# Attention and a four-expert layer from a build-time planner: softmax sums in a flow of their own, one region for P, one exponential per bank

## The chip, the cores and the metric

The kernel runs on one core of one Trainium2 chip. The metric is the device time of one execution in microseconds (us), as the median of the runs shown. It is a single launch; all arrays lie in device memory before and after it, and everything is 32-bit.

## What is computed

```python
q_pool = q.reshape(B, H, S // 2, 2, D).mean(axis=3)        # B=8, H=8, S=1152, D=64
attn = softmax(scale * q_pool @ k.T)                       # 576 queries x 1152 keys per head
x = (attn @ v) -> [B, 576, 512]
logits = x @ w_gate;  w = softmax of the two best of E=4 experts
for e in range(E):                                         # each expert: causal attention
    a = softmax(causal(scale * (x@wq[e]) @ (x@wk[e]).T))   # 576 x 576, head size 64
    out += (row's weight for e) * (a @ (x@wv[e]) @ wo[e])
```

## The kernel before

**Stages.** The 64 heads are worked in 32 head pairs (`p`), the two heads of a pair side by side: one in rows 0 to 63 of TensorE's array, one in rows 64 to 127. The 576 queries of a pair are two blocks (`QB`: 256 and 320), its 1152 keys nine chunks of 128 (`NKC`). For each pair the kernel

- loads K in three pieces (512, 512 and 128 columns, `f_loadk`), splits it into a high part by a cast on ACT and a low part by a subtraction on POOL (`f_prepk`), and does the same to Q;
- finds row maxima from the high parts alone: products of 512 columns into PSUM (`f_max`, `f_mxs`), reduced on DVE (`row_max`, L635);
- computes scores keys-by-queries with four products per chunk and head (high by high, low by high, high by low, and a row of ones times the negated maxima; `rows2`, L378), and takes `exp` of them from PSUM into tiles called `pt` (this is P, L725, `f_st`). A bank of 512 columns holds two chunks of the 256-query block or one chunk of the 320-query block; each chunk and head has an ACTIVATE of its own;
- multiplies P by V (`f_av`, `cols2`, L385: two matmuls a head, the heads in different columns of the array) and adds the chunk's P into the P of chunk 0 (`sacc`), so that the sum over keys needs one reduction at the end. The addition is issued in the same step as the product: on POOL (`add_up`, L397), or, if the planner's clock of POOL is over 3.0 us (`OFP`) behind and DVE's is not behind, as a folding reduction on DVE into a small tile (`fold_in`, `fold32`, L776; at most three for one block). The `pt` tile is freed behind the addition;
- at the end of a block folds the sum, inverts it through a small product (L823), scales and writes the pair's x in a high and a low part (`g_norm`, `g_split`, `f_xfin`).

After four pairs a batch's x is complete, and its experts' part starts: projections (`f_qk`, `f_vproj`, L369, all 128 rows and columns of the array), maxima (`f_mmax`), scores by chunk and query block (`f_mst`), P by V (`f_mav`) and the output product (`f_out`). In `f_mst`, for every batch but the last, chunk 1 is multiplied twice: 128 columns for queries 128 to 255 (packed in one bank with chunk 0) and 320 columns for block 1.

**Order.** The instruction order of every engine is fixed at build time by a list planner. Each stage is a Python generator (a "flow") that yields the time from which its next step can run and, for PE steps, a mode: A for products on 64-row halves (L378), B for P by V and the sums' small product (64-column halves), C for full products (L369). `emit` advances one model clock per engine. At each step the loop at the end picks a flow: what continues the present mode if it is ready within a tolerance, else by `pref()`, else what is ready first. The rules are the rows of `PLAN`: one row per half pair (65 rows, 16 numbers each). Columns 1 and 2 are how many us PE may wait for a score step or a P-by-V step (column 1 mostly 0.3 to 0.6); columns 3 and 4 are counts of waiting P-by-V steps from which mode B goes before mode C, and from which such a step has no extra 3 us. The set that is counted (`wait_av`) holds for each block only its next chunk, since only that one is asked.

**Buffers.** `pt` is a ring of 20 tiles of 2 x 320 columns, each with a tag of its own; K arrives in three 512-column tiles (`kraw`), which also take the 128-column piece; x has five buffers, and from the sixth chunk (`XG`) of a pair its x buffer must be had. PSUM's eight banks are one ring (`gen`).

Of the kernel before, what the change touches and what calls it, by code (L numbers as in the profile page):

```python
# [14 lines left out]
NB = 8  # L15
# [16 lines left out]
NPT, NKH = 20, 6  # L32
SWC = 0.8
NSL, OFP, OFD = 4, 3.0, 0.0
# [13 lines left out]
WST, WSP, WPR = 1.0, 0.2, 4  # L48
XG = 6
# [129 lines left out]
class Kept(Ring):  # L179
# [5 lines left out]
    def new(self):  # L185
        t = min(self.slots)
        self.slots.remove(t)
        self.live += 1
        r = Res(self.aps[t[3]], self)
        _, r.u, r.ue, r.slot = t  # L190
        return r

# [16 lines left out]
def pooled_attention_then_moe_kernel(ctx: ExitStack, tc: tile.TileContext, qT, kT, vP, wall, wop, out):  # L209
# [78 lines left out]
    r_x = ring("x", [128, 2, SQ], F32R, 5)  # L288
# [146 lines left out]
    KH, KL, QH, QL = {}, {}, {}, {}  # L435
    KT = lambda p: ((0, 384), (384, 384), (768, 384)) if p == 0 else ((0, 512), (512, 512), (1024, 128))
# [22 lines left out]
    wait_av, go = set(), [0]  # L459

    def av_need(key, *t):
        if key not in wait_av:
            wait_av.add(key)
# [10 lines left out]
    def av_prio():  # L474
        return 1.5 if cut[0] == "B" else 2.5 if len(wait_av) >= row(4) else 4.5
# [13 lines left out]
    def f_loadk(p, t):  # L489
        yield lambda: max(r_kraw.avail(), sp())  # L490
        k = r_kraw.new()
        a, n = KT(p)[t]
        mv(k[:, :n], kT[p, :, a:a + n], [], [k])
# [15 lines left out]

    def load_first():  # L510

        ks, (q, q1), qh, ql = [r_kraw.new() for _ in range(3)], [r_qraw.new() for _ in range(2)], r_qh.new(), r_ql.new()
# [805 lines left out]
```

## Time and profile before

| | |
|---|---|
| median of 3 runs | 1123.16 us (1123.04 to 1123.74) |
| span of the profiled execution | 1123.1 us |
| PE / DVE / POOL / ACT busy | 1092.6 / 875.7 / 874.4 / 651.9 us |
| first matmul to last | starts 7 us after the first instruction, ends 5 us before the last |

Busy times are the union of an engine's instructions in the profiled execution; the span is from its first instruction to its last, and nothing is added around it, since span and median agree to 0.1 us. A matmul's recorded duration holds its way through the array as well, so that neighbours overlap, and the distance from one start to the next tells what it costs.

### The profile page before, as it was taken

Reading aid. Unit: us, or ns where it says so; the run is one execution under the profiler, and the core shown is the slowest. Engines: PE = TensorE matmul, PEld = TensorE weight load, DVE = VectorE, ACT = ScalarE, POOL = GpSimd, SP = SyncE. Lnnn points to the kernel's source line nnn. Section 1 sums busy time; section 2 is a strip of 40 time slices with the busy share of each in tenths; the row PEclk is TensorE's granted clock in tenths of the full one; section 3 lists DMA queues with packets and bytes.
Section 4 is the critical chain, followed back from the end, with each engine's and each line's share of the span. In section 5 each row is a group of like instructions: output and inputs, shape, how many; then the busy total and the mean of one; then the engine's idle time right before and its main releaser. Section 6 shows DMA issues by size and latency. Waiting matters only on the chain.

```text
span 1123.1 us, 29516 instructions
## 1 busy us (share of the span) xinstructions
PE 1092.6 (97%) x11184; PEld 878.3 (78%) x11184; DVE 875.7 (78%) x2055; ACT 651.9 (58%) x2036; POOL 874.4 (78%) x808
## 2 busy tenths in 40 slices
PE   7998999999999999999999999999999999999997
PEld 5876798777987779778787778877787877987785
DVE  8999878787688776978578787788768887677885
ACT  5765637666375654657456674567645766456543
POOL 5898948999299991999939998399965999468812
PEclk9998999999999999999999999999999999999999
DMA  7332321223113122221322023230232203200011
GB/s 186 92 100 80 78 52 52 65 65 84 33 55 75 34 74 70 63 57 33 100 69 73 23 73 88 59 84 4 74 88 74 65 2 108 58 23 2 2 39 48
DMA packets 46398, 70.31 MB, mean 63 GB/s; under 512 B 7216, under 2 KB 25648, under 8 KB 46256
## 3 DMA queue, kind: packets, MB, share of 16 engines
q1 hardware_dynamic: 41648, 59.15, 17.2%
q0 software_dynamic: 4464, 9.14, 5.6%
q8 instruction: 88, 1.44, 0.5%
q14 instruction: 54, 0.44, 0.1%
q10 hardware_dynamic: 144, 0.13, 0.0%
HBM read 58.73 MB, written 9.44 MB: 61 GB/s over the span
## 4 chain that ended last, share of the span: by engine, by line
PE 70%; POOL 12%; DVE 11%; issue 2%; DMA 2%; ACT 2%; SPq 0%; POOLq 0%; DVEq 0%; ACTq 0%
PE gen L378 31%; PE gen L369 20%; PE gen L385 19%; POOL pt L397 10%; DVE PM L635 5%; DVE part L776 2%; DMA qraw<-in_qT 2%; POOL pt L1125 1%; DVE gen L1062 1%; POOL kl L397 1%; ACT pt L725 1%; PE gen L823 1%; DVE WL L393 1%; DVE gate L977 1%; DMA kraw<-in_kT 0%
## 5 line engine op out<-in xcount | busy, mean ns | idle before, releaser
L397 POOL TENSOR_TENSOR pt<-pt,pt 128x512 f32<-128x512 f32 (+4 forms) x488 | 667.7, 1374 | 40.5 <-PE gen L385 5.1
L635 DVE TENSOR_REDUCE PM<-gen 128x1 f32<-128x512 f32 (+3 forms) x678 | 407.8, 658 | 132.2 <-PE gen L378 107.4
L725 ACT ACTIVATE pt<-gen 128x320 f32<-128x320 f32 (+1 forms) x1152 | 371.6, 446 | 63.0 <-PE gen L378 56.3
L385 PE MATMUL gen<-pt,v 128*64 128x320 f32 (+4 forms) x2752 | 346.7, 403 | 2.0 <-POOL pt L1125 1.5
L385 PEld LDWEIGHTS gen<-pt,v 128*64 128x64 f32 (+1 forms) x2752 | 189.0, 137 | 127.9 <-issue 7.4
L378 PE MATMUL gen<-qh,kh 64*128 64x320 f32 (+1 forms) x1152 | 229.8, 312 | 4.8 <-DVE PM L635 2.5
L378 PE MATMUL gen<-qh,kl 64*128 64x320 f32 (+1 forms) x1152 | 218.1, 299 | 0.0
L378 PE MATMUL gen<-ql,kh 64*128 64x320 f32 (+1 forms) x1152 | 210.6, 293 | 0.0
L378 PE MATMUL gen<-RM,ON 64*128 64x320 f32 (+1 forms) x1152 | 210.4, 292 | 0.0
L378 PEld LDWEIGHTS gen<-qh,kh 64*128 64x128 f32 x1152 | 155.8, 186 | 28.1 <-ACT pt L725 7.3
L776 DVE TRANSPOSE_TENSOR_REDUCE part<-pt 128x20 f32<-128x640 f32 (+1 forms) x188 | 143.4, 781 | 27.5 <-POOL pt L397 27.2
L378 PE MATMUL gen<-kh,qh 64*128 64x512 f32 (+2 forms) x768 | 149.4, 374 | 11.2 <-ACT qh L389 7.1
L378 PEld LDWEIGHTS gen<-RM,ON 64*128 64x128 f32 x1152 | 149.6, 187 | 0.0
L378 PEld LDWEIGHTS gen<-ql,kh 64*128 64x128 f32 x1152 | 149.3, 186 | 0.0
L378 PEld LDWEIGHTS gen<-qh,kl 64*128 64x128 f32 x1152 | 146.1, 186 | 2.8
L397 POOL TENSOR_TENSOR kl<-kraw,kh 128x512 fp32r<-128x512 f32 (+2 forms) x96 | 103.0, 1104 | 21.0 <-PE gen L378 16.7
L378 PEld LDWEIGHTS gen<-kh,qh 64*128 64x128 f32 x768 | 88.3, 189 | 29.9 <-issue 11.2
L369 PE MATMUL gen<-x,WH 128*128 128x320 f32 (+1 forms) x512 | 105.0, 299 | 0.0
L977 POOL TENSOR_TENSOR gate<-v,gate 128x20 f32<-128x20 f32 x7 | 1.6, 225 | 123.9 <-DVE gate L977 123.9
L369 PEld LDWEIGHTS gen<-x,WH 128*128 128x128 f32 x512 | 81.9, 188 | 4.2 <-issue 1.9
L1062 DVE CUSTOM_DVE_ANT_0 gen<-gen,mqk 64x288 f32<-64x288 f32 (+4 forms) x160 | 74.3, 504 | 9.6 <-PE gen L378 8.4
L389 ACT COPY accs<-gen 128x256 f32<-128x256 f32 (+1 forms) x96 | 39.1, 407 | 70.6 <-PE gen L385 70.5
(117 smaller groups left out, 1523.3 us busy)
## 6 DMA issues: line engine op xcount, KB each, us to landing
v<-in_vP SPq DMA_DIRECT2D x96, 192.0 KB
kraw<-in_kT SPq DMA_DIRECT2D x62, 256.0 KB
qraw<-in_qT SPq DMA_DIRECT2D x31, 288.0 KB
qraw<-in_qT POOLq DMA_DIRECT2D x31, 288.0 KB, 4.5
out<-ob SPq DMA_DIRECT2D x28, 256.0 KB
kraw<-in_kT SPq DMA_DIRECT2D x31, 64.0 KB
RM<-nt SPq DMA_DIRECT2D x124, 1.2 KB
wst<-in_wall SPq DMA_DIRECT2D x8, 193.0 KB
```

Source lines behind the costliest of these rows:

```text
L369: nc.tensor.matmul(o, lhsT, rhs, start=start, stop=stop)
L378: nc.tensor.matmul(o(j), l(HEAD[j]), r(HEAD[j]), start=i == 0, stop=i == len(terms) - 1)
L385: nc.tensor.matmul(o(HEAD[j]), l(j), r(j), start=start, stop=stop)
L389: nc.scalar.copy(o, i)
L393: nc.vector.tensor_tensor(o, a, b, op=op)
L397: nc.gpsimd.tensor_tensor(o, a, b, op=op)
L635: nc.vector.tensor_reduce(pm[:, i:i + k, t], ps[:, :n * k].rearrange("p (c n) -> p c n", c=k), axis=AX.X, op=ALU.max)
L725: nc.scalar.activation(pts[i][:, j, :qn], st[j][:, qn * i:qn * i + qn], AF.Exp, scale=0.0625)
L776: nc.vector.tensor_reduce(out, src.rearrange("p a (b r) -> p a b r", r=32), axis=AX.X, op=ALU.add, apply_transpose=True)
L823: nc.tensor.matmul(den[HEAD[j], 400:400 + k], fold, part[:, m, j * k:j * k + k], start=True, stop=True)
L977: f(*a, **kw)
L1062: nc.vector.tensor_tensor_reduce(p, p, mqk[:m, 384 + m - w:384 + m], 1.0, LOW, ALU.add, ALU.max, pm[:m, j, c, i:i + 1])
```

## The change

1. `pt` becomes one region `PT` of 18 places. A score step of two chunks takes two neighbouring places, and one ACTIVATE per bank writes both (512 columns). A step of one chunk takes a single place, by preference one without free neighbours.
2. The additions into `sacc` are a flow of their own (`f_sum`). It starts when a block's first P-by-V product has been planned, and each addition is planned when the planner's POOL clock less column 16, or its DVE clock plus column 17, is reached; the earlier of the two engines takes it (DVE only while its small tile has room). A place is freed when both its product and its addition are planned.
3. In `f_mst` (all batches but the last) chunk 1 is multiplied once, 448 columns for queries 128 to 575, and its P goes to both blocks.
4. x has six buffers instead of five, and is demanded from the eighth chunk; the 128-column piece of K has a `kraw` tile of its own; the high part of a weight is cast 1.5 us (`WSM`) later in the plan than its arrival.
5. `pend` counts all P-by-V steps that wait, not the next of each block; a P-by-V step's place in its block is the order in which its scores were made.
6. `PLAN` has 65 new rows of 18 numbers. Column 1 is mostly 0.02 to 0.3; columns 3 and 4 run from 2 to 15 and from 1 to 10 (4 or 5 and 4 or 5 in many rows of the first half); column 16 is 0.5 to 3, column 17 from -1.5 to 1.5.

```diff
-NPT, NKH = 20, 6
+NPT, NKH = 18, 6
-NSL, OFP, OFD = 4, 3.0, 0.0
+NSL = 4
-WST, WSP, WPR = 1.0, 0.2, 4
-XG = 6
+WST, WSP, WPR, WSM = 1.0, 0.2, 4, 1.5
+XG = 8
 PLAN = [
-    (0.05, 0.45, 0.45, 5, 2, 2.0, 0.25, 0.02, 4, 4.5, 2.9, 4.05, 4.1, 6, 99, 0),
...
+    (0.15, 0.3, 0.1, 15, 5, 1, 0.02, 0.1, 3, 4.5, 2.9, 4.05, 4.75, 3, 1.5, 1, 0.5, 0.5),
...
+class Places(Kept):
...
+    def new2(self):
+        i = min(self.pairs())[1]
+        return [self.take(i), self.take(i + 1)]
+
+    def one(self, now):
+        ok = [x for x in self.slots if x[0] <= now] or [min(self.slots)]
+        free = {x[3] for x in self.slots}
+        lone = lambda x: (x[3] - 1 in free) + (x[3] + 1 in free)
+        return self.take(min(ok, key=lambda x: (lone(x), x))[3])
...
-    r_pt = ring("pt", [128, 2, 320], F32, NPT)
+    PT = cst.tile([128, NPT, 2, 320], F32, name="PT")
+    r_pt = Places([PT[:, i] for i in range(NPT)])
-    r_kraw = ring("kraw", [128, 512], F32, 3)
+    r_kraw = {n: ring(f"kraw{n}", [128, n], F32, b) for n, b in ((512, 3), (128, 1))}
-    r_x = ring("x", [128, 2, SQ], F32R, 5)
+    r_x = ring("x", [128, 2, SQ], F32R, 6)
...
-        if cut[0] == "B" or go[0] > 0 or tail_now():
+        if cut[0] == "B" or tail_now():
             return t
-        return t if len(wait_av) >= row(4) else t + 3.0
+        return t if pend[0] >= row(4) else t + 3.0
...
+    def st_unit(p, hf, cs):
...
+        pts = r_pt.new2() if len(cs) == 2 else [r_pt.one(clk["PE"])]
...
+        n, a = qn * len(cs), pts[0].slot
+        for j in range(2):
+            nc.scalar.activation(PT[:, a:a + len(cs), j, :qn], st[j][:, :n].rearrange("p (i q) -> p i q", q=qn),
+                                 AF.Exp, scale=0.0625)
...
     def f_av(p, c, hf, pt):
+        if k == 0:
+            SACC[key], SUMS[key] = pt, NKC - 1
+        else:
+            spawn("sum", f_sum(key, pt, 0, n, n))
+        pend[0] += 1
...
-        if c and not fold_in(sacc, pt, n):
-            add_up(sacc, pt, 0, n, n, pool_tt)
-        if c:
-            pt.free()
+        if k:
+            used(pt)
...
+    def f_sum(key, pt, f, qn, full):
+        sacc, n = SACC[key], qn - f
+        last = key[0] == NB - 1 and len(key) == 3
+        folds = lambda: len(key) == 2 and r_part_ok(sacc)
+        p_at, d_at = lambda: clk["POOL"] - row(16), lambda: clk["DVE"] + row(17) if folds() else INF
+        yield lambda: max(pt.rw, min(p_at(), d_at())) if av_next.get(key, 0) else INF
+        if p_at() <= d_at():
+            o = sacc[:, :, f:full]
+            (any_tt if last else pool_tt)(o, o, pt[:, :, f:full], ALU.add, 2 * n, [pt], [sacc])
+        else:
...
+            fold32(part[:, part.m, :2 * k].rearrange("p (a b) -> p a b", a=2), pt[:, :, :n], 2 * n, [pt], [part])
+            part.m += 1
+        SUMS[key] -= 1
+        used(pt)
+
+    def r_part_ok(sacc):
+        part = PARTS.get(sacc)
+        return part.m < NSL if part else r_part.avail() <= clk["DVE"]
...
+    def mst_groups(qb):
+        if qb is None:
+            return [[(0, 0, 256, [(0, 0)])], [(1, 128, 576, [(0, 128), (1, 0)])], [(0, 256, 576, [(1, 0)])],
+                    [(2, 256, 576, [(1, 0)])], [(3, 384, 576, [(1, 128)]), (4, 448, 576, [(1, 256)])]]
...
-            yield lambda: on(True, w.rw, act())
+            yield lambda: on(True, w.rw + WSM, act())
...
-            return "ABC" if len(wait_av) >= row(3) else "ACB"
+            return "ABC" if pend[0] >= row(3) else "ACB"
```

## Rows read from the trace of the kernel before

**Rows 1.** The page: busy time, share and instructions of each engine; the chain that ended last, by engine.

```profile
PE 1092.6 (97%) x11184; PEld 878.3 (78%) x11184; DVE 875.7 (78%) x2055; ACT 651.9 (58%) x2036; POOL 874.4 (78%) x808
...
PE 70%; POOL 12%; DVE 11%; issue 2%; DMA 2%; ACT 2%; SPq 0%; POOLq 0%; DVEq 0%; ACTq 0%
```

**Rows 2.** Waits of PE's weight loads, over the whole span: who waited for whom, us in total, times, longest. A load runs ahead of the matmuls, so not all of it is lost.

```profile
PEld gen L378 <- ACT pt L725: 9.5, 35, 1.0
PEld gen L378 <- DVE PM L635: 9.2, 24, 2.2
PEld gen L823 <- ACT part L818: 8.1, 17, 1.5
...
PEld gen L369 <- ACT pt L725: 3.5, 15, 0.3
...
PEld gen L378 <- ACT kh L389: 3.4, 4, 2.1
PEld gen L369 <- DVE PM L635: 2.9, 6, 1.6
PEld gen L385 <- ACT pt L725: 2.2, 8, 0.4
...
PEld gen L823 <- ACT pt L725: 1.3, 5, 0.4
```

**Rows 3.** Waits of DVE for POOL, and of ACT for K's arrival, over the whole span; same columns.

```profile
DVE part L776 <- POOL pt L397: 27.2, 30, 3.7
...
ACT kh L389 <- DMA kraw<-in_kT: 22.2, 20, 3.6
```

**Rows 4.** Timeline of PE from 211 us on, experts' scores: start us, us, instruction, count. Chunks of 320 columns, the 64-key chunk 4, and chunks 0 and 1 of block 0.

```profile
212.22 0.31 PE L378 MATMUL gen<-mqh,mkh 64*128 64x320 f32 x2
...
212.80 0.25 PE L378 MATMUL gen<-mqh,mkh 64*128 64x192 f32 x2
...
213.22 0.22 PE L378 MATMUL gen<-mqh,mkh 64*64 64x128 f32 x2
...
213.46 0.33 PE L378 MATMUL gen<-mqh,mkh 64*128 64x256 f32 x2
...
213.99 0.22 PE L378 MATMUL gen<-mqh,mkh 64*128 64x128 f32 x2
...
214.38 0.45 PE L378 MATMUL gen<-kh,qh 64*128 64x512 f32 x2
```

**Rows 5.** Groups of instructions by line and shape: count, busy us (union), mean ns of one, idle before. The exponentials of 320 and of 256 columns, and ACT's copies out of PSUM of 512 and of 256.

```profile
L725 ACT ACTIVATE pt<-gen 128x320 f32<-128x320 f32 x576 | 206.0, 477 | 12.6 <-PE gen L378 10.4 <-PE gen L369 0.3 <-ACT part L818 0.2
L725 ACT ACTIVATE pt<-gen 128x256 f32<-128x256 f32 x576 | 169.8, 415 | 50.4 <-PE gen L378 45.9 <-POOL pt L397 3.2 <-ACT pt L725 0.4
...
L389 ACT COPY ob<-gen 128x512 f32<-128x512 f32 x31 | 18.2, 587 | 25.1 <-PE gen L369 22.9 <-ACT gate L977 0.9 <-ACT part L818 0.7
...
L389 ACT COPY accs<-gen 128x256 f32<-128x256 f32 x48 | 18.1, 377 | 10.9 <-PE gen L385 10.8
```

**Rows 6.** The same view: the additions on POOL, the folds and the row maxima on DVE, the P-by-V products.

```profile
L635 DVE TENSOR_REDUCE PM<-gen 128x1 f32<-128x512 f32 x558 | 350.1, 681 | 120.5 <-PE gen L378 103.5 <-PE gen L369 15.7
L397 POOL TENSOR_TENSOR pt<-pt,pt 128x640 f32<-128x640 f32 x207 | 325.2, 1572 | 15.5 <-ACT part L818 3.6
L397 POOL TENSOR_TENSOR pt<-pt,pt 128x512 f32<-128x512 f32 x239 | 314.2, 1315 | 18.8 <-PE gen L385 4.1
...
L776 DVE TRANSPOSE_TENSOR_REDUCE part<-pt 128x20 f32<-128x640 f32 x123 | 99.0, 825 | 15.3 <-POOL pt L397 15.0
```

**Rows 7.** Busy us (and instructions) of PE, PEld, DVE, ACT and POOL, granted clock, and DMA share and GB/s, in 90 to 100 us.

```profile
90.00:100.00 10.00, 6.26 (x61) 5.29 (x61) 10.00 (x14) 5.05 (x17) 9.54 (x7) 0.73 0.37 114
```

**Rows 8.** Timeline of 92 to 98 us, all engines: what ACT, PE and DVE did there, with the idle time before in brackets.

```profile
93.09 0.62 ACT L389 CAST OH<-wst 128x512 fp32r<-128x512 f32 x1 [2.07 <-DMA wst<-in_wop]
...
93.62 0.42 ACT L389 COPY accs<-gen 128x320 f32<-128x320 f32 x1
93.94 2.31 ACT L725 ACTIVATE pt<-gen 128x256 f32<-128x256 f32 x8
94.09 0.50 PE L378 MATMUL gen<-kh,qh 64*128 64x512 f32 x1 [1.74 <-ACT accs L389]
...
97.16 0.58 PE L378 MATMUL gen<-qh,kh 64*128 64x256 f32 x1 [1.93 <-DVE PM L635]
```

**Rows 9.** Timeline of PE at two changes between modes: from A to B at 176 us, and from B to A at 185 us.

```profile
176.34 0.34 PE L378 MATMUL gen<-mkh,mqh 64*128 64x384 f32 x2
176.61 0.65 PE L385 MATMUL gen<-pt,v 128*64 128x256 f32 x4
...
185.73 0.50 PE L378 MATMUL gen<-kh,qh 64*128 64x512 f32 x2
186.06 0.28 PE L378 MATMUL gen<-qh,kh 64*128 64x256 f32 x2
```

**Rows 10.** The chain that ended last, in order of time: start us, us, what, count. P-by-V stretches at the beginning and the end of the steady part.

```profile
177.45 8.35 PE gen L385 x68
...
994.73 8.35 PE gen L385 x68
```

**Rows 11.** The page's costliest groups: the P-by-V matmuls, all shapes.

```profile
L385 PE MATMUL gen<-pt,v 128*64 128x320 f32 (+4 forms) x2752 | 346.7, 403 | 2.0 <-POOL pt L1125 1.5
```

More of the change, by code (lines that the diff above doesn't have):

```diff
@@ L191, in new, with pairs, pair, take @@
         return r
+class Places(Kept):
+    def pairs(self):
+        at = {x[3]: x for x in self.slots}
+        return [(max(at[i], at[i + 1]), i) for i in at if i + 1 in at]
+    def pair(self):
+        p = self.pairs()
+        return min(p)[0][0] if p else INF
+    def take(self, i):
+        t = next(x for x in self.slots if x[3] == i)
+        self.slots.remove(t)
+        self.live += 1
+        r = Res(self.aps[i], self)
+        _, r.u, r.ue, r.slot = t
+        return r
+    def new2(self):
[6 more added lines that the diff above has]
+        return self.take(min(ok, key=lambda x: (lone(x), x))[3])
 class Flow:
@@ L456, in rdy, with av_need @@
         return 0.0 if clk[eng] >= t - 0.02 else t
[L459 to L463, printed above, removed]
+    def av_need(*t):
         t = max((0.0,) + t)
@@ L474, in av_prio @@
     def av_prio():
-        return 1.5 if cut[0] == "B" else 2.5 if len(wait_av) >= row(4) else 4.5
+        return 1.5 if cut[0] == "B" else 2.5 if pend[0] >= row(4) else 4.5
     def den_prio():
@@ L489, in f_loadk @@
     def f_loadk(p, t):
-        yield lambda: max(r_kraw.avail(), sp())
-        k = r_kraw.new()
         a, n = KT(p)[t]
+        yield lambda: max(r_kraw[n].avail(), sp())
+        k = r_kraw[n].new()
         mv(k[:, :n], kT[p, :, a:a + n], [], [k])
@@ L510, in load_first @@
     def load_first():
-        ks, (q, q1), qh, ql = [r_kraw.new() for _ in range(3)], [r_qraw.new() for _ in range(2)], r_qh.new(), r_ql.new()
+        ks, (q, q1), qh, ql = [r_kraw[512].new() for _ in range(3)], [r_qraw.new() for _ in range(2)], r_qh.new(), r_ql.new()
         qs, sl = [Res(None) for _ in Q0], [slice(a, b) for a, b in Q0]
@@ L583, in f_prepk, with g_low @@
             spawn_max(p)
-        yield lambda: on(True, r_kl[big(n)].avail(), kh.rw, pool())
-        kl = r_kl[big(n)].new()
-        pool_tt(kl[:, :n], k[:, :n], kh[:, :n].bitcast(F32), ALU.subtract, n, [k, kh], [kl])
-        KL[p, t] = kl
+        yield from g_low(p, t, k, kh)
         k.free()
+    def g_low(p, t, k, kh):
+        n = KT(p)[t][1]
+        yield lambda: on(True, r_kl[n].avail(), kh.rw, pool())
+        kl = r_kl[n].new()
+        pool_tt(kl.ap, k.ap, kh.bitcast(F32), ALU.subtract, n, [k, kh], [kl])
+        SH[p, t], SL[p, t] = kh, kl
     def f_max(p):
@@ L632, in f_mxs, with drop_kh @@
             rows_of(p)
+        if ("max2", p) in flag:
+            drop_kh(p)
+    def drop_kh(p):
+        for t in range(3):
+            KH.pop((p, t))
     def row_max(pm, i, k, t, n, ps):
@@ L694, in f_rows @@
         flag.update(flags)
+    UNITS = [(hf, range(c, min(c + k, NKC))) for hf, k in ((0, 2), (1, 1)) for c in range(0, NKC, k)]
+    av_seq = {}
     def f_st():
@@ new lines, in f_st @@
+            for hf, cs in UNITS:
+                if p not in X and hf * NKC + cs[-1] >= XG:
+                    yield lambda: 0.0 if p in X else r_x.avail()
+                    take_x(p)
+                ok = lambda: all((p, tof(p, c)) in SH for c in cs) and p in QL and ("row", p, hf) in flag
+                yield (lambda: on(True, pt_need(cs), r_gen.avail(2), clk["ACT"] - row(14),
+                                  *(SL[p, tof(p, c)].rw for c in cs), QL[p].rw, RM[p % 2].rw) if ok() else INF, "A")
+                st_unit(p, hf, cs)
@@ new lines, in pt_need @@
+    def pt_need(cs):
+        return r_pt.pair() if len(cs) == 2 else r_pt.avail()
+    def st_unit(p, hf, cs):
+        q0, qn = QB[hf]
+        qc, rm = slice(q0, q0 + qn), RM[p % 2]
+        pts = r_pt.new2() if len(cs) == 2 else [r_pt.one(clk["PE"])]
+        qh, ql, st = QH[p], QL[p], [r_gen.new() for _ in range(2)]
+        for i, c in enumerate(cs):
+            t = tof(p, c)
+            kh, kl, o = SH[p, t], SL[p, t], 128 * c - KT(p)[t][0]
+            kc = slice(o, o + 128)
+            terms = [(lambda r: kh[r, kc], lambda r: qh[r, qc]), (lambda r: kl[r, kc], lambda r: qh[r, qc]),
+                     (lambda r: kh[r, kc], lambda r: ql[r, qc]),
+                     (lambda r: ON[r], lambda r: rm[r, q0 + r.start:q0 + qn + r.start])]
+            rows2(lambda j: st[j][:, qn * i:qn * i + qn], terms, [kh, kl, qh, ql, rm], st)
+        n, a = qn * len(cs), pts[0].slot
+        for j in range(2):
+            nc.scalar.activation(PT[:, a:a + len(cs), j, :qn], st[j][:, :n].rearrange("p (i q) -> p i q", q=qn),
+                                 AF.Exp, scale=0.0625)
+            emit("ACT", n / 1200 + 0.055, [st[j]], pts, late=0.05)
+        for x in st:
+            x.free()
+        for i, c in enumerate(cs):
+            t = tof(p, c)
+            st_done[p] += 1
+            ks_done[p, t] = ks_done.get((p, t), 0) + 1
+            if ks_done[p, t] == KT(p)[t][1] // 64:
+                SH.pop((p, t)).free()
+                SL.pop((p, t)).free()
+            av_seq.setdefault((p, hf), []).append(c)
+            spawn("av", f_av(p, c, hf, pts[i]), av_prio)
+        prog["f"] = sum(st_done.values()) / (2 * NKC)
+        if st_done[p] == 2 * NKC:
@@ L770, in f_av, with used @@
             V.pop((p, c // 3)).free()
-        if c == NKC - 1:
-            spawn("xfin", f_xfin(p, hf, ACC.pop((p, hf)), SACC.pop((p, hf))))
+        if k == NKC - 1:
+            spawn("xfin", f_xfin(p, hf, ACC.pop(key), SACC[key]))
+    def used(pt):
+        if pt in half:
+            half.discard(pt)
+            pt.free()
+        else:
+            half.add(pt)
+    def f_sum(key, pt, f, qn, full):
[7 more added lines that the diff above has]
+            (any_tt if last else pool_tt)(o, o, pt[:, :, f:full], ALU.add, 2 * n, [pt], [sacc])
+        else:
+            part = PARTS.get(sacc)
+            if part is None:
+                part = PARTS[sacc] = r_part.new()
+                part.m = 1
+            k = n // 32
+            fold32(part[:, part.m, :2 * k].rearrange("p (a b) -> p a b", a=2), pt[:, :, :n], 2 * n, [pt], [part])
[3 more added lines that the diff above has]
+    def r_part_ok(sacc):
+        part = PARTS.get(sacc)
+        return part.m < NSL if part else r_part.avail() <= clk["DVE"]
     def fold32(out, src, n, R, W):
@@ L778, in fold32, with g_norm @@
         emit("DVE", n * 0.00112 + 0.054, R, W)
[L780 to L802 removed]
+    def g_norm(key, acc, sacc, n, box, gate=None):
         yield lambda: rdy("ACT", r_accs.avail(), acc.rw)
@@ L806, in g_norm @@
         acc.free()
-        yield lambda: rdy("DVE", sacc.rw, 0.0 if sacc in PARTS else r_part.avail())
+        yield lambda: rdy("DVE", sacc.rw, 0.0 if sacc in PARTS else r_part.avail()) if SUMS[key] == 0 else INF
+        SACC.pop(key)
         k = n // 32
@@ L858, in f_xfin @@
         q0, qn = QB[hf]
-        yield from g_norm(acc, sacc, qn, box)
+        yield from g_norm((p, hf), acc, sacc, qn, box)
         accs, den = box
@@ L1072, in f_mmax @@
               lambda: -1)
+    def mst_groups(qb):
+        if qb is None:
+            return [[(0, 0, 256, [(0, 0)])], [(1, 128, 576, [(0, 128), (1, 0)])], [(0, 256, 576, [(1, 0)])],
+                    [(2, 256, 576, [(1, 0)])], [(3, 384, 576, [(1, 128)]), (4, 448, 576, [(1, 256)])]]
+        q0, qn = QB[qb]
+        f = lambda c: max(0, 128 * c - q0)
+        return packed([(c, q0 + min(f(c), qn - 128), q0 + qn, [(qb, f(c))]) for c in range((q0 + qn - 1) // 128 + 1)],
+                      lambda x: x[2] - x[1])
     def f_mst(b, ep, pt):
@@ L1115, in f_mst @@
-        if q0 + qn == SQ:
+        for g in mst_groups(pt if tail else None):
+            ds = [(i, qb, f) for i, (_, _, _, to) in enumerate(g) for qb, f in to]
+            yield (lambda: on(("mr", b, ep, pt) in flag and (("v", b, g[-1][0]) if tail else ("g", b, 0)) in flag
+                              and min(lows.get((b, m), 0) for m in (ep, 2 + ep)) > (pt if tail else 1),
+                              r_pt.avail(len(ds)), r_gen.avail(2), kl.rw, ql.rw, rm.rw), "A")
+            pts, st, o = [r_pt.one(clk["PE"]) for _ in ds], [r_gen.new() for _ in range(2)], 0
+            if g[-1][0] == 4:
+                nc.vector.memset(pts[-1][64:128, :, 256:320], 0.0)
+                emit("DVE", 0.13, [], [pts[-1]])
+            at = []
+            for c, x, y, _ in g:
+                kn = min(128, SQ - 128 * c)
+                kc, qc = slice(128 * c, 128 * c + kn), slice(x, y)
+                rows2(lambda j: st[j][:kn, o:o + y - x],
+                      [(lambda r: kh[r, kc], lambda r: qh[r, qc]), (lambda r: kl[r, kc], lambda r: qh[r, qc]),
+                       (lambda r: kh[r, kc], lambda r: ql[r, qc]), (lambda r: ON[r, :kn], lambda r: rm[r, qc])],
+                      [kh, kl, qh, ql, rm], st)
+                at.append(o - x)
+                o += y - x
+            for j in range(2):
+                for (i, qb, f), pt_ in zip(ds, pts):
+                    q0, qn = QB[qb]
+                    kn, o = min(128, SQ - 128 * g[i][0]), at[i] + q0
+                    nc.scalar.activation(pt_[:kn, j, f:qn], st[j][:kn, o + f:o + qn], AF.Exp, scale=0.125)
+                    emit("ACT", (qn - f) / 1200 + 0.055, [st[j]], [pt_], late=0.05)
+            for j in range(2):
+                st[j].free()
+            for (i, qb, f), pt_ in zip(ds, pts):
+                c = g[i][0]
+                m_prog[b] += 0.48
+                if 128 * c >= QB[qb][0]:
+                    spawn("mask", f_mask(b, ep, qb, c, pt_, f, min(128, SQ - 128 * c)))
+                else:
+                    spawn("mav", f_mav(b, ep, qb, c, pt_), av_prio)
@@ L1116, in f_mst @@
+        if not tail or pt:
             flag.add(("mst", b, ep))
@@ L1136, in f_mav @@
         key = (b, ep, qb)
-        yield (lambda: av_need((*key, c), pt.rw, vr.rw, 0.0 if c else r_gen.avail())
+        if c == 0:
+            SACC[key], SUMS[key] = pt, cl
+            for x in wait_sum.pop(key, ()):
+                spawn("sum", f_sum(key, *x))
+        elif key in SACC:
+            spawn("sum", f_sum(key, pt, f, qn, qn))
+        else:
+            wait_sum.setdefault(key, []).append((pt, f, qn, qn))
+        pend[0] += 1
+        yield (lambda: av_need(pt.rw, vr.rw, 0.0 if c else r_gen.avail())
                if av_next.get(key, 0) == c else INF, "B")
-        wait_av.discard((*key, c))
+        pend[0] -= 1
         if c == 0:
             ACC[key] = r_gen.new()
-            SACC[key] = pt
         av_next[key] = c + 1
-        acc, sacc = ACC[key], SACC[key]
+        acc = ACC[key]
         n = qn - f
```

132 lines of the change are left out of this document (22 added, 110 removed), and 128 rows, old and new, of the table PLAN.

## The prediction

> **What bounds the kernel now.** The page comes first: PE is busy for 97% of the span, DVE and POOL for 78%, ACT for 58%, and 70% of the chain that ended last is PE [rows 1]. So an engine beside PE matters only where PE waits for it, and a gain has two sources alone: less PE work, or fewer of its waits and mode changes. "97%" hides some waits, because a matmul's recorded end overlaps the next one; the list of waits shows them better. Its weight loads waited 9.5 + 3.5 + 2.2 + 1.3 = 16.5 us for exponentials, 9.2 + 2.9 = 12.1 us for DVE's row maxima (PSUM banks not yet reduced), 8.1 us for the sums' last small step on ACT, 3.4 us for K's cast [rows 2]. That is some 40 us, spread thinly: the longest single wait is 2.2 us. One place stands out, 90 to 100 us, where PE is busy for 6.26 of 10 us and the granted clock is 0.73 [rows 7]. P by V runs in long stretches of 68 matmuls, early and late alike [rows 10]; at four matmuls a chunk that is 17 chunks, nearly the whole ring of 20.
>
> **The sum** starts from the profiled execution, a span of 1123.1 us, which is also the runs' median (1123.16) to 0.1 us. A difference of 0.2%, 2.2 us, is about the least that a measurement of this kernel can tell from none.
>
> **Chunk 1 of the experts in one product.** A score product is four pairs of matmuls. The four 128-column pairs take from 213.99 to 214.38, 0.39 us; four 320-column pairs from 212.22 to 212.80, 0.58 us [rows 4]. Put on the end of a 320-column pair, 128 columns would cost 0.58 x 128/320 = 0.23 us. So 0.16 us goes each time, in 7 batches and 2 expert pairs: 14 x 0.16 = **-2.2 us**. All of it is PE's own work on the path. At the other end, the 64-key chunk 4 had 128 columns for 0.24 us (213.22 to 213.46 [rows 4]), by which nothing is saved: 0 to -2.2, and I take the -2.2, since the removed product is the very shape of 213.99. Exponentials, masks and additions of chunk 1 keep their number.
>
> **One exponential a bank.** Two of 256 columns become one of 512 in 4 steps x 2 heads x 32 pairs = 256 banks. One of 256 adds 169.8/576 = 0.295 us to ACT's busy time, one of 320 adds 206.0/576 = 0.358 us [rows 5]. No exponential of 512 was run. By the slope between these two it costs 0.295 + 0.063 x 4 = 0.55 us; by that of the copies out of PSUM, 587 - 377 = 210 ns for 256 more columns [rows 5], 0.505 us. The saving per bank is 0.59 less that, 0.04 to 0.085 us, so 10 to 22 us of ACT. ACT is not the bound; only its lag counts. In a two-chunk step ACT works 4 x 0.295 = 1.18 us, PE 8 pairs of 256 columns, at 0.58/4 x 256/320 = 0.116 each 0.93 us: ACT falls 0.25 us behind. In a one-chunk step it is 0.72 against 0.58: 0.14 behind. Per pair that is 4.5 x 0.25 = 1.1 and 9 x 0.14 = 1.3, so just under half of the 16.5 us, some 7.5, comes from the steps that change, and they lose 0.08 to 0.17 of their 0.25. That gives -2.4 to -5.1; I take **-3.5 us**, bounds 0 to -8. The first of two chunks is now ready later by up to one exponential's share, 0.25 us; a stretch of P by V begins with chunks that are older than that, so this costs nothing as long as the stretches stay long.
>
> The Trainium skill ("ScalarE: Activation LUTs", section "What ACT_TABLE_LOAD costs") gives 186 ns + 0.833 ns a column for an ACTIVATE, of which some 93 ns overlap with a neighbour. This case's 415 ns for 256 columns agrees with 399 by that rule, while 62 ns for 64 more columns is steeper than its 53. By it a bank saves 93 ns, and this term would be -5.5 instead of -3.5 us.
>
> **Sums as a flow.** Now the additions come in the same step as the products. A stretch of 17 products takes 8.35 us [rows 10], and 17 additions of 1.3 to 1.57 us [rows 6] are 22 to 27 us of POOL; folds take up to three a block at 0.825 us. DVE then stands behind POOL: 27.2 us in 30 waits for the last addition, before the closing fold [rows 3], and what is queued behind that fold on DVE are row maxima of 0.68 us [rows 6], whose banks PE needs. After the change an addition is planned when an engine is near it, also ahead of its own product, and the two engines are filled evenly. If DVE's waits for POOL fall by half, DVE gains 13 us of 876, and PE's 12.1 us for row maxima shrink. I take **-5 us**. Bounds: all 12.1 us go, or +5 us, since a place is now held until both its uses are planned and there are 18, not 20. An addition still starts no earlier than its block's first product, so with long stretches POOL's work stays bunched. What is late next is ACT.
>
> **Weights, K, x.** At 93 us ACT's cast of a weight waited 2.07 us for its DMA; queued behind it were `accs` and eight exponentials, and PE sat idle for 1.74 and, behind DVE, for 1.93 us [rows 8]. Casting 1.5 us later in the plan takes away most of the first: **-2 us**, bounds 0 to -3.7 (the idle time of that window). K's 128-column piece no longer occupies a 512-column tile: ACT's 22.2 us of waits for K [rows 3] are mostly hidden, PE's share is 3.4 [rows 2]; **-1.5 us**, 0 to -3.4. The DMA's bytes stay. The sixth x buffer I cost at nothing: in these rows no wait is for x. It only loosens the planner.
>
> **The new rules.** `pend` counts all waiting chunks, and columns 3 and 4 are often 4 or 5, so P by V may start with fewer chunks, and PE waits less for a score step (column 1: 0.2 us instead of 0.3 to 0.6). Each stretch costs a change into B and one out of it. From A to B the pair of 384 columns takes 0.27 us to the next start, where its rate gives 0.174: 0.10 more. From B to A, the first 512-column pair takes 0.33 for 0.23: 0.10 more [rows 9]. There are 2752/4 = 688 products of a chunk [rows 11]; at 17 a stretch some 40 stretches. If stretches shrink to 13, 53: 13 x 0.2 = **+3 us** (estimate; bounds 0, and +26 for stretches of four).
>
> Sum: -2.2 - 3.5 - 5 - 2 - 1.5 + 3 = -11.2, so 1123 - 11 = **1112 us**.
>
> **Rivals.**
> - *More of the waits go.* If the new rules, together with the above, remove most of the 16.5 + 12.1 + 3.4 us and the 3.7 us of rows 7, 36 us in all, with the 2.2 us, and switches stay as they are, the floor is about 1085; two thirds of it give 1098. For it: the waits are many and short, which a planner with better balance can fill. Against: the row maxima need DVE for 0.68 us a bank in any order.
> - *The waits only move.* PE waits for whichever of ACT, DVE and POOL is last; take one away and the next is near (DVE and POOL both at 78%). Then only the merged product counts: 1121.
> - *Short stretches: slower.* Place: the choice of mode after a score step that is not ready. If columns 3 and 4 make P by V start at four chunks, there are 172 stretches, 132 more, +26 us, against -14 from the other terms: 1135. It decides from 14/0.2 = 70 more stretches, that is below 688/110 = 6 chunks each. For: 4 or 5 stand in many of the new rows. Against: mode A is left only when no step of A is ready, and once in B all ready chunks are taken.
> - *The region is not what it seems.* If waits were kept for `PT` as a whole, exponentials would stand behind every P-by-V stretch, with ACT idle in all 40 of them, up to 40 x 8.35 = 334 us: some 1450. The slices are disjoint; hardly likely.
>
> The Trainium skill ("TensorEngine Tiling (Array Packing)", section "Key Properties") says that a change of tiling mode drains the engine. The trace agrees, 0.10 us at each of the two changes shown, and it is this rule that speaks against the change: under the short-stretch rival it would make it slower.
>
> **Chances.** The sum as worked out, 1103 to 1120: 0.50. More waits gone, about 1098: 0.20. Waits only move, 1121 to 1125: 0.12. Short stretches, about 1135: 0.16. The region: 0.02. Faster by over 0.2% (below 1120.9): 0.72, that is the first two and a little of the third; within 0.2%: 0.10; slower: 0.18. The range leaves out some 0.07 below and 0.13 above: 1094 to 1127.
>
> **What would show it.** Right: 896 exponentials in scores instead of 1152, 256 of them 512 wide with some 0.5 us each; no 128-column score products in the first seven batches; waits of PE for ACT's exponentials well below 16.5 us, of DVE for POOL below 27.2; no hole at 90 to 100 us; P-by-V stretches of 40 or more matmuls. Wrong: many stretches of 16 to 24 matmuls; more waits for `pt` places; folds in front of row maxima, with PE's waits for L635 above 12.1 us.

## The result, and the profile after

The changed kernel takes **1092.31 us** (1091.49 to 1092.65) against 1123.45 for the kernel before, run beside it: a ratio of 0.9712, interval 0.9697 to 0.9728. That is 31 to 32 us less, where 11 were forecast, and 1.7 us below the forecast's range. The profiled execution spans 1090.9 us. One execution of a kernel further down, flat_x5, took 3031.65 us and is left out of its figure.

The page of the changed kernel: busy time and count by engine, and the chain that ended last.

```profile
PE 1071.2 (98%) x11072; PEld 863.5 (79%) x11072; DVE 908.5 (83%) x2130; ACT 635.1 (58%) x1780; POOL 802.2 (74%) x756
PE 83%; DVE 7%; POOL 5%; ACT 2%; issue 2%; DMA 1%; SPq 0%; POOLq 0%; ACTq 0%; DVEq 0%
```

Beside [rows 1]: 112 matmuls and 256 ACT instructions are gone, 72 us of POOL have gone, and 33 us of DVE have come. POOL, 12% of the chain before, is 5% of it now; PE is 83% instead of 70%. The kernel is more nearly what its PE work alone would take.

Waits of PE's weight loads in the changed kernel (us, times, longest), and of DVE for POOL. L409 is the old L378, L416 the old L385, L400 the old L369, L886 the old L823, L675 the old L635, L770 the old L725 and L860 the old L776.

```profile
PEld gen L409 <- DVE PM L675: 9.3, 23, 1.0
...
PEld gen L886 <- ACT part L881: 4.7, 10, 0.7
PEld gen L416 <- ACT PT L770: 4.4, 17, 0.3
...
PEld gen L400 <- DVE PM L675: 2.2, 7, 0.5
...
PEld gen L400 <- ACT PT L770: 1.7, 7, 0.3
...
PEld gen L409 <- ACT PT L770: 0.5, 2, 0.3
```

```profile
DVE part L860 <- POOL PT L428: 33.9, 29, 4.5
```

Against [rows 2]: waits for exponentials were 16.5 us and are 6.6; those for row maxima are as many (11.5 after 12.1), but the longest is 1.0 instead of 2.2; those for the closing sum went from 8.1 to 4.7. DVE waits for POOL not less but more, 33.9 us after 27.2 [rows 3].

Distances from start to start tell where the gain lies. Take for each matmul the distance to the next start, less its columns at the rate of its mode (0.455 ns a column for a pair of heads in A; 0.417 and 0.455 ns a column for each matmul in B and C, where 320 columns of P by V take 0.133 us and 512 of C 0.232). What is left over sums to 133.6 us before and 101.5 after. The columns are as many in both kernels, since 448 are 128 and 320, so these 32.1 us are the whole gain: 23.9 of them are in A, 6.8 in B, 1.5 in C. The listed waits of the loads make up less than half of it: without those on "issue" they sum to 66.9 us before and 54.6 after.

Counted at the same number of columns done, the changed kernel is 6 us ahead behind the hole of [rows 7] and gains most of the rest from 350 us on. Changes of mode, counted along PE's order, rose from 195 to 210. P by V comes in 58 stretches instead of 49, of 11.9 chunks on average instead of 14.0; 19 of the 58 still have 17 or 18 chunks, and those under ten rose from 11 to 24.

The merged chunk and the new exponentials: PE's timeline at an experts' score step, and ACT's groups by shape.

```profile
252.33 0.37 PE L409 MATMUL gen<-mqh,mkh 64*128 64x448 f32 x2
252.54 0.36 PE L409 MATMUL gen<-mqh,mkl 64*128 64x448 f32 x2
252.74 0.36 PE L409 MATMUL gen<-mql,mkh 64*128 64x448 f32 x2
252.94 0.37 PE L409 MATMUL gen<-MRM,ON 64*128 64x448 f32 x2
253.14 0.32 PE L409 MATMUL gen<-mqh,mkh 64*128 64x320 f32 x2
```

```profile
L770 ACT ACTIVATE PT<-gen 128x320 f32<-128x320 f32 x576 | 205.4, 491 | 37.1 <-PE gen L409 31.1 <-DVE part L877 4.2 <-POOL PT L428 0.8
...
L770 ACT ACTIVATE PT<-gen 128x512 f32<-128x512 f32 x256 | 137.3, 603 | 40.0 <-PE gen L409 35.9
```

Four 448-column pairs take 0.81 us, as the sum had it (0.58 + 0.23). An exponential of 512 adds 137.3/256 = 0.536 us, inside the bounds 0.505 to 0.55 and nearer to the upper one.

### The profile page after: what moved, and what is told of

Read it like the earlier page. It is cut to its first block, busy times and chain, and to the rows that moved or that the text cites. A ratio compares the mean times of both kernels' runs of the same rounds, so it can differ in the third digit from the quotient of the medians.

```text
span 1090.9 us, 29049 instructions
## 1 busy us (share of the span) xinstructions
PE 1071.2 (98%) x11072; PEld 863.5 (79%) x11072; DVE 908.5 (83%) x2130; ACT 635.1 (58%) x1780; POOL 802.2 (74%) x756
## 4 chain that ended last, share of the span: by engine, by line
PE 83%; DVE 7%; POOL 5%; ACT 2%; issue 2%; DMA 1%; SPq 0%; POOLq 0%; ACTq 0%; DVEq 0%
PE gen L409 35%; PE gen L416 26%; PE gen L400 21%; POOL PT L428 3%; DVE PM L675 3%; DVE part L860 1%; ACT PT L770 1%; PE gen L886 1%; DMA qraw<-in_qT 1%; POOL ql L428 1%; ACT PT L1174 0%; DVE gen L901 0%; POOL PT L1195 0%; DVE gate L1040 0%; POOL kl L428 0%
## 5 line engine op out<-in xcount | busy, mean ns | idle before, releaser
L428 POOL TENSOR_TENSOR PT<-PT 128x640 f32<-128x640 f32 (+4 forms) x436 | 596.4, 1378 | 59.9 <-PE gen L886 10.5
L675 DVE TENSOR_REDUCE PM<-gen 128x1 f32<-128x512 f32 (+3 forms) x678 | 408.4, 658 | 78.6 <-PE gen L409 62.3
L770 ACT ACTIVATE PT<-gen 128x320 f32<-128x320 f32 (+2 forms) x896 | 358.0, 517 | 79.2 <-PE gen L409 69.0
L416 PE MATMUL gen<-PT,v 128*64 128x320 f32 (+4 forms) x2752 | 348.7, 402 | 0.8 <-POOL PT L1195 0.8
L416 PEld LDWEIGHTS gen<-PT,v 128*64 128x64 f32 (+1 forms) x2752 | 184.8, 137 | 123.7 <-issue 5.9
L409 PE MATMUL gen<-qh,kh 64*128 64x320 f32 (+1 forms) x1152 | 208.2, 306 | 3.1 <-DVE PM L675 2.4
L860 DVE TRANSPOSE_TENSOR_REDUCE part<-PT 128x16 f32<-128x512 f32 (+1 forms) x249 | 182.2, 757 | 34.5 <-POOL PT L428 33.9
L409 PE MATMUL gen<-qh,kl 64*128 64x320 f32 (+1 forms) x1152 | 200.4, 294 | 0.0
L409 PE MATMUL gen<-RM,ON 64*128 64x320 f32 (+1 forms) x1152 | 197.9, 292 | 0.3 <-DMA RM<-nt 0.3
L409 PE MATMUL gen<-ql,kh 64*128 64x320 f32 (+1 forms) x1152 | 197.9, 292 | 0.0
L409 PEld LDWEIGHTS gen<-qh,kh 64*128 64x128 f32 x1152 | 142.7, 185 | 18.6 <-DVE PM L675 5.8
L409 PE MATMUL gen<-kh,qh 64*128 64x512 f32 (+2 forms) x768 | 139.4, 367 | 7.7 <-ACT qh L420 7.1
L409 PEld LDWEIGHTS gen<-qh,kl 64*128 64x128 f32 x1152 | 135.0, 185 | 3.2
L409 PEld LDWEIGHTS gen<-RM,ON 64*128 64x128 f32 x1152 | 137.0, 186 | 0.5 <-issue 0.5
L409 PEld LDWEIGHTS gen<-ql,kh 64*128 64x128 f32 x1152 | 136.4, 185 | 0.0
L400 PE MATMUL gen<-x,WH 128*128 128x320 f32 (+1 forms) x512 | 104.5, 299 | 0.0
L409 PEld LDWEIGHTS gen<-kh,qh 64*128 64x128 f32 x768 | 81.6, 188 | 23.5 <-issue 7.9
L400 PEld LDWEIGHTS gen<-x,WH 128*128 128x128 f32 x512 | 81.9, 188 | 4.1 <-issue 1.4
L400 PE MATMUL gen<-x,WL 128*128 128x320 f32 (+1 forms) x256 | 75.4, 295 | 0.0
```

Source lines behind the costliest of these rows:

```text
L400: nc.tensor.matmul(o, lhsT, rhs, start=start, stop=stop)
L409: nc.tensor.matmul(o(j), l(HEAD[j]), r(HEAD[j]), start=i == 0, stop=i == len(terms) - 1)
L416: nc.tensor.matmul(o(HEAD[j]), l(j), r(j), start=start, stop=stop)
L428: nc.gpsimd.tensor_tensor(o, a, b, op=op)
L675: nc.vector.tensor_reduce(pm[:, i:i + k, t], ps[:, :n * k].rearrange("p (c n) -> p c n", c=k), axis=AX.X, op=ALU.max)
L770: nc.scalar.activation(PT[:, a:a + len(cs), j, :qn], st[j][:, :n].rearrange("p (i q) -> p i q", q=qn), AF.Exp, scale=0.0625)
```

## The experiments

Times are given as ratios to the kernel before, run beside each; for differences, 0.001 is 1.125 us, since the kernel before took 1124.9 to 1125.5 us in these groups. The intervals are about +-0.0015, so a difference of two is good to some 2 us.

**The parts, in the order of the changed kernel.** The planner issues instructions and moves its clocks separately, so an instruction can be altered while the plan stays the same.

```diff
-            nc.scalar.activation(PT[:, a:a + len(cs), j, :qn], st[j][:, :n].rearrange("p (i q) -> p i q", q=qn), AF.Exp, ...)
+            for i in range(len(cs)):
+                nc.scalar.activation(PT[:, a + i, j, :qn], st[j][:, qn * i:qn * i + qn], AF.Exp, scale=0.0625)
```

> The changed kernel, planned as it is, but each two-chunk bank read by two exponentials of 256 columns again instead of one of 512: 256 more ACT instructions and the same order on every engine. Theory A (the gain is in the parts themselves: fewer, longer instructions): ACT is back to 58 to 60% busy and PE's waits for exponentials go from some 7 us back towards 16.5, so 6 to 10 us more, 1098 to 1102. Theory B (the gain is in the order that the rules and flows give; the same work is worth little by itself): at most 3 us more, 1092 to 1095.

Measured 0.9747 (1096.5 us): 3.9 us more, between the two theories' figures. PE's waits for exponentials in that kernel (its L771 is the L770 above):

```profile
PEld gen L416 <- ACT PT L771: 5.2, 20, 0.3
...
PEld gen L409 <- ACT PT L771: 2.8, 12, 0.5
PEld gen L400 <- ACT PT L771: 2.3, 9, 0.4
```

They are 10.3 us after 6.6, a step of the size of the time lost; ACT is busy for 647.8 us instead of 635.1, 0.050 us for each of the 256 banks.

```diff
-                rows2(lambda j: st[j][:kn, o:o + y - x], ...)            # x to y, 448 columns
+                    for s, at0 in ((slice(x, x + 128), o), (slice(x + 128, y), o + 128)):
+                        ...                                               # the same four terms, 128 and 320 columns
```

> The changed kernel, planned as it is, but the experts' 448-column products issued as 128 + 320 columns into the same bank: 112 more matmuls, the same order otherwise. By my sum 14 x 0.16 = 2.2 us more (1094.5); theory A and B agree on it. If the 64-row rate of the rows holds, nothing.

Measured 0.9727 (1094.4 us): 1.7 us more, near the 2.2 of the sum, though by itself not clear of the interval.

```diff
+    def behind(pt, issue):
+        issue() if pt in multiplied else kept.setdefault(pt, []).append(issue)
...
-            (any_tt if last else pool_tt)(o, o, pt[:, :, f:full], ALU.add, 2 * n, [pt], [sacc])
...
+                behind(pt, lambda: nc.gpsimd.tensor_tensor(o, o, pt[:, :, f:full], op=ALU.add))
+                emit("POOL", 2 * n * 0.0024 + 0.1, [pt], [sacc])
```

> The changed kernel, planned as it is, but an addition that the planner puts ahead of its own P-by-V product is issued right behind that product: 102 of 582 additions move back in POOL's or DVE's queue, PE's and ACT's order stays. My term for the sums as a flow rested on such early additions: if that is right, 2 to 5 us more (1094 to 1097) and DVE's waits for POOL above 33.9 us. Rival: the additions' place in the queue matters little to PE, within 1 us.

Measured 0.9802 (1103.0 us): 10 us more, where 2 to 5 were expected. The weight loads' waits for the closing sum in that kernel (the old L823 is L904 here), and DVE's for POOL at the closing fold:

```profile
PEld gen L904 <- ACT part L899: 14.5, 15, 3.2
```

```profile
DVE part L878 <- POOL PT L856: 35.8, 29, 4.5
```

4.7 us became 14.5. These waits are at the end of a block, where the last additions now come late and PE reaches the small product before its input is there. Row maxima do not suffer (8.4 us of waits for L675 after 9.3), and DVE waits little longer for POOL (35.8 after 33.9). So in this order early additions matter through the closing chain, not through DVE's row maxima as the prediction had it. Much of the 10 us is one place near the end of the kernel; at the same number of columns done the lag is 4.6 us at 1020 us and 11.5 at 1085. Stretches of this kernel there (busy us and count of PE, PEld, DVE, ACT, POOL, granted clock, DMA share, GB/s):

```profile
1020.00:1030.00 10.00, 8.79 (x107) 6.77 (x103) 5.27 (x13) 4.74 (x18) 9.61 (x9) 1.00 0.00 1
1030.00:1040.00 10.00, 8.12 (x75) 4.90 (x75) 6.64 (x14) 4.83 (x15) 9.50 (x10) 1.00 0.01 2
1040.00:1050.00 10.00, 9.59 (x58) 9.30 (x59) 4.47 (x13) 2.55 (x9) 2.21 (x2) 0.66 0.00 0
```

PE idles for 3.1 us in the first two, and the granted clock is 0.66 in the third.

**The hole of the kernel before.**

```diff
-            yield lambda: on(True, w.rw, act())
+            yield lambda: on(True, w.rw + 1.5, act())
```

> The kernel before with one edit: the high part of a weight is cast 1.5 us later in the plan, nothing else. My term: the hole at 90 to 100 us closes, 2 us less (1121; at most 3.7 less). Rival: also the stretch at a low granted clock behind the hole goes, 5 to 7 us less (1117). Other rival: DVE's splits of the weights (1.5 us each) hold PE there anyway, no change.

Measured 0.9962 (1120.9 us): 4.3 us less. The hole at 90 to 100 us in this kernel, for [rows 7]:

```profile
90.00:100.00 10.00, 9.79 (x133) 8.91 (x132) 9.63 (x17) 8.90 (x30) 9.61 (x7) 1.00 0.17 48
```

PE is busy for 9.79 instead of 6.26 us, and the granted clock is 1.00 instead of 0.73: with the idle stretch the time at the lower of the two levels (1.2 and 2.4 GHz) went as well, which the -2 us had left out. At the same number of columns done, this kernel is 6.8 us ahead right behind the hole and 4.5 at the end. So the hole was worth more than the 3.7 us of idle time that bounded the term, and the order that shifted behind it gave some of that back.

**Is it the parts or the table?**

```diff
-SWC = 0.8
+SWC = 0.81
```

> The changed kernel with one number of the planner's model moved by a hair: the time it assumes for issuing the accumulating DMA on POOL (SWC) is 0.81 instead of 0.80 us. No instruction is added or removed; only the order that the planner finds can differ. Theory A (gain in the parts): the time stays within 5 us of 1092. Theory B (the table is fitted to one order, step by step): the later rows meet another state than the one they were chosen for, and most of what the order gave is lost: 1115 to 1135.

Measured 1.0041 (1129.4 us): 37 us are lost by 0.01 us in the planner's model, and the kernel is slower than the one before. Theory B holds here. Up to 348 us PE's order is the same (a few neighbours trade places on ACT, DVE and POOL at 123 and 257 us) and the two kernels keep the same times to within 1 us. From there on the orders differ, and the rows meet states that they were not chosen for: the same matmul of the order comes 25 us later at 800 us, mode changes rise from 210 to 265, and the closing sum's waits from 4.7 to 14.1 us.

> The kernel before with the same kind of nudge (SWC 0.82 instead of 0.80). If its table is as brittle as the new one, it loses its whole 20.6 us (1146); I expect half, 1130 to 1138, since its rows are the same over long stretches.

Measured 1.0094 (1134.8 us): 10.6 us lost, about half, as expected. Each table had one nudge, so that the older one is less brittle is likely but not shown.

> The changed kernel with the rows of the kernel before (columns 16 and 17 filled with 1.5 and 0.5 everywhere): the structure with rules fitted to another order. Theory A: near 1095 to 1100. Theory B: slower than the kernel before, 1125 to 1145.

Measured 1.0077 (1133.6 us): the structure under the other kernel's rows is slower than before. Their columns 3 and 4 were chosen for the old count of waiting steps, so this tells more of the fit than of the structure.

**The structure without fitting.** `PLAN` is 65 times one row: (0.05, 0.2, 0.1, 15, 4, 1.2, ...) for the changed kernel, (0.05, 0.6, 0.2, 6, 2, 1.2, ...) for the kernel before.

> The changed kernel with one and the same row for all 65 half pairs (each column's most frequent value in its table): the parts and flows without fitting. With the next run this splits the gain: if the structure (flows, pairs, six x) is worth something by itself, this is 10 us or more faster than the kernel before with one flat row; if it is all fitting, the two are level. I expect 1120 to 1130 here.

> The kernel before with one and the same row for all 65 half pairs (each column's most frequent value in its own table). Expected 1135 to 1150: its own table is worth 10 to 25 us, that of the changed kernel 25 to 40.

Measured 0.9984 (1123.5 us) and 1.0188 (1146.2 us). The structure with its own flat row is 0.0204, 23 us, faster. The two rows differ and come out of the fitted tables, so some of the 23 us may be the better row; the flat kernels with rows exchanged were not run. Against its flat row the old table is worth 21 us (1.0188 to 1), the new one 31 (0.9984 to 0.9712).

**The same search for both.** Each kernel's table was found anew by random changes, row by row, with the same number of tries; the planner's own end time decided, the chip measured.

> The kernel before with a table fitted anew: from its flat row, front to back, 40 random changes tried for each of the 65 rows, the best by the planner's own end time kept (2600 tries). If fitting alone made the gain: as fast as refit_after. If the structure makes it: near its own table's time, 1120 to 1125.

> The changed kernel with a table fitted anew from its flat row by the same search with the same 2600 tries. If the structure is worth 10 us or more at equal fitting: 1108 to 1115, 8 to 15 us faster than refit_before; the rest to 1092 is then the longer search behind its own table. If only the fitting counts: 1120 to 1125, level with refit_before.

Measured 0.9973 (1122.0 us) and 0.9843 (1107.0 us). At equal fitting the structure is worth 0.0130, 14.6 us. This is one search for each kernel, and how far apart two searches of one kernel end was not tried. Another 0.0131, 14.7 us, separates this refit from the table of the change. DVE's waits for POOL, and the loads' for row maxima and for the closing sum, in the refitted kernel before, and then in the refitted changed kernel:

```profile
DVE part L776 <- POOL pt L397: 41.2, 36, 6.8
...
PEld gen L378 <- DVE PM L635: 14.1, 38, 1.1
...
PEld gen L823 <- ACT part L818: 6.0, 20, 0.9
...
PEld gen L369 <- DVE PM L635: 3.2, 7, 1.4
```

```profile
DVE part L860 <- POOL PT L428: 36.4, 30, 5.3
...
PEld gen L886 <- ACT part L881: 8.0, 17, 1.9
...
PEld gen L409 <- DVE PM L675: 5.4, 21, 0.5
...
PEld gen L400 <- DVE PM L675: 0.4, 2, 0.2
```

Waits for row maxima fall from 17.3 to 5.8 us, which is what the prediction hoped of the sums. But DVE's waits for POOL fall by an eighth, not by half, and those for the closing sum rise from 6.0 to 8.0.

**One part at a time, flat.** Each of these is the changed kernel with its flat row and one part as before; compare with flat_after, 0.9984. The order changes with the part, and by how much the order alone moves the time of a flat kernel was not measured; the "some 4 us" below is a guess. So small figures are no more than a sign.

```diff
-            return "ABC" if pend[0] >= row(3) else "ACB"
+            return "ABC" if waiting() >= row(3) else "ACB"      # waiting(): blocks with a step open
...
```

> The changed kernel with one flat row (as flat_after, 1123.5 us) and the old way of counting waiting P-by-V steps: only the next of each open block, so that the flat row's thresholds of 15 and 4 are hardly ever met. With a flat row nothing is fitted to one order, so the difference to flat_after is this part's own; a flat plan is uncertain by some 4 us from small differences of order. If starting P by V early is what keeps PE from waiting: 6 to 12 us more (1130 to 1136), with fewer, longer P-by-V stretches. Rival (my prediction's view that early starts only cost changes of mode): the same or less.

Measured 1.0091 (1135.1 us): 12 us more, with 57 P-by-V stretches instead of 62. One place has the size of the whole loss: at the same number of columns done this kernel is 11 us behind at 70 us, and between 6 and 13 us behind from there on. Two stretches of 10 us in this kernel (columns as above), and then in flat_after:

```profile
30.00:40.00 10.00, 8.54 (x66) 5.72 (x62) 9.97 (x22) 6.21 (x18) 3.93 (x3) 0.94 0.41 117
40.00:50.00 10.00, 9.87 (x48) 5.85 (x50) 9.96 (x19) 0.00 (x0) 6.01 (x6) 0.55 0.21 32
```

```profile
30.00:40.00 10.00, 10.00 (x109) 7.87 (x107) 9.82 (x21) 9.21 (x26) 9.82 (x8) 1.00 0.26 70
40.00:50.00 10.00, 10.00 (x129) 8.43 (x127) 9.56 (x18) 7.03 (x17) 8.75 (x7) 1.00 0.67 186
```

With the old count P by V waits until the 18 places are full. PE is left with row maxima, which DVE paces; it issues 66 and 48 matmuls in 10 us instead of 109 and 129, the granted clock falls to 0.55, and ACT does nothing at all from 40 to 50 us. From 43 us on 72 P-by-V matmuls, 18 chunks, come in one stretch. What this shows is the old count under thresholds of 15 and 4, which were chosen for the new one; the old count under the old flat row's 6 and 2 was not tried in this kernel, so the 12 us are not the count's alone.

> The changed kernel with one flat row and each addition issued in the step of its product again, by the rule of the kernel before (DVE if POOL is 3 us behind). My term for the sums as a flow, 5 us: 1128. sums_behind_products says 10: 1133. Rival: that was only the damage to a fitted order, 0 to 3.

Measured 1.0042 (1129.8 us): 6.5 us more, so near the 5 us of the term. DVE's waits for POOL, and the loads' for row maxima and for the closing sum, in this kernel (its L902 is the L886 of flat_after), and then in flat_after:

```profile
DVE part L876 <- POOL PT L428: 36.3, 26, 6.6
...
PEld gen L409 <- DVE PM L675: 7.3, 21, 1.2
...
PEld gen L902 <- ACT part L897: 6.0, 12, 2.3
```

```profile
DVE part L860 <- POOL PT L428: 20.1, 24, 2.2
...
PEld gen L886 <- ACT part L881: 9.6, 17, 1.6
...
PEld gen L409 <- DVE PM L675: 5.2, 19, 0.6
```

Here the flow does work as predicted: DVE waits 20.1 us for POOL instead of 36.3, and waits for row maxima are shorter, while those for the closing sum are longer. That is the other way round from the held order.

> The changed kernel with one flat row, five x buffers and x demanded from the sixth chunk, as before. My prediction cost the sixth buffer at nothing: 1123 (within 4). Rival: the experts' projections may be spread over a longer time only with the sixth, 5 to 8 us more (1129 to 1131), with the mode C work in longer lumps.

Measured 1.0011 (1126.7 us): 3 us more, which the order alone may well do; neither side is shown.

> The changed kernel with one flat row and two exponentials of 256 columns a bank again, which the planner knows of. By two_exp_same_order 4 us more (1127); by the planner's leave to move other work around it, 3 to 8 more.

Measured 1.0026 (1127.7 us): 4.7 us more, near the 3.9 of the held order.

> The changed kernel with one flat row and the experts' chunk 1 in two products, grouped as before (128 columns beside chunk 0; 320 by itself). By split_chunk1_same_order 1.7 us more than flat_after (1125); with the order free, 0 to 6 more.

Measured 1.0050 (1129.8 us): 7.4 us more, where the held order gave 1.7. The other 5.7 us come with the order and the different grouping, so a flat difference of 3 to 7 us need not be the part's own.

K's own 128-column tile, 18 against 20 places, and the order of P by V within a block were not taken out singly.

## Why the prediction was wrong

Right in direction, near in most parts, wrong in size. The step that failed is **"the new rules", +3 us**: it priced the rules by their changes of mode and put what they gain at nothing.

- *Chunk 1, -2.2 us.* 1.7 in the held order: consistent, though within the uncertainty.
- *One exponential a bank, -3.5 us.* 3.9 in the held order, 4.7 flat. Right, by PE's waits for ACT as foreseen. The bank's saving (0.59 - 0.536 = 0.054 us) is close to the 0.04 that the slope between 256 and 320 columns gave. The Trainium skill ("ScalarE: Activation LUTs", section "What ACT_TABLE_LOAD costs") has back-to-back ACTIVATEs overlap by some 93 ns; this trace shows 54 ns a bank, and the measurement decides. The times, each good to some 2 us, can't tell -3.5 from the -5.5 of that rule.
- *Sums as a flow, -5 us.* 6.5 flat, 10 in the held order, much of that in one place near the end. The size is near; the path stays open. In the change itself DVE's waits for POOL did not halve, they rose from 27.2 to 33.9 us, and in the held order it is PE's wait for the closing sum that the early additions save (4.7 us; 14.5 without them). Flat, DVE's waits for POOL and PE's for row maxima fall as predicted, and those for the closing sum rise.
- *Weights, -2 us.* 4.3 at the end (2.6 to 6.0 by its interval) and 6.8 right behind the hole, above the bound of 3.7; the stretch at the lower clock went with the idle time.
- *Sixth x, 0.* About 3 flat, not clear of the uncertainty. *K, -1.5:* not tried singly. PE's waits for K's cast fell from 3.4 us to 0.6, but they are 0.8 in flat_before too, which has the old tiles.
- *The new rules, +3 us.* The base of the price was wrong: the kernel before had 49 stretches of 14.0 chunks, not 40 of 17, which was read from two of them. The price itself stayed small: 15 more changes of mode, where 13 more stretches would have made 26; at the 0.10 us of [rows 9] that is 1.5 us. What was left out is what the rules gain. From the table of equal fitting to the table of the change it is 14.7 us, with nothing else edited. Taken from the other end, the three parts in the held order and the cast come to 1.7 + 3.9 + 10 + 4.3 = 20 us of the 31, so some 11 are left for the rules where +3 was forecast. Both readings have their weak side (one search for each kernel; parts taken out of a fitted order), but they agree in sign and nearly in size. The new table is also fitted further than the old one, 31 us above its flat row against 21, and that appears in no row of the kernel before. The count of all waiting chunks belongs here as well: under its flat row it is worth 12 us, because P by V starts before the ring is full. The full-ring stretches stood in [rows 10], and I read them as thrift. That such a stretch can leave ACT idle is shown in flat_old_count; for the kernel before it is not shown.

That the other terms sum to -14 us and the structure leads by 14.6 at equal fitting is partly luck: the parts by themselves measured more than their terms, and the structure also holds the new count.

The rival "more of the waits go" (1098, floor 1085) was the nearest, at a chance of 0.20. "Short stretches" did not come as priced: stretches became shorter by two chunks on average, not by thirteen, and 1.5 us of added changes weigh little beside the rest. "The waits only move" is refuted by the 31 us.

## What to carry to other kernels

Where a build-time planner with a fitted rule table sets the order, a row of the trace tells what a part costs, but not what a better fit will find: bound it by the floor (work plus unavoidable changes), and leave the range open towards it. Compare structures at equal fitting (both flat, and both refitted with the same tries), and test parts in a held order. Taking a part out of a fitted plan and planning anew measures the damage to the plan as well (37 us for a change of 0.01 us in the model). Long runs of one kind of product are cheap for PE's switches and can be dear for the engines that idle meanwhile, as ACT did for 10 us before the stretch of 72 matmuls.

## What the runs showed that was not expected

A wait of 2 us on a weight's DMA, with 3.7 us of PE idle time behind it, also brought the granted clock to 0.73 for that stretch [rows 7]; without the wait it stayed at 1.00, and the kernel gained 4.3 us. In flat_old_count a stretch in which PE issued 48 matmuls in 10 us had a granted clock of 0.55, so mostly the lower of the two levels, although the profile counts PE as busy for 9.87 of the 10 us. Near the end of sums_behind_products 3.1 us of idle time in 20 us were followed by 10 us at 0.66.
